# Turning q and k with 64x64 products on four quarters of the array, k loaded in whole rows, in an attention and feed-forward kernel with a re-sequenced plan

## The chip, the cores and the metric

The kernel runs on one core of a Trainium2 chip. The metric is the device time of one execution in microseconds (us). Before the change, three runs gave 1478.62, 1480.76 and 1485.36 us; the median is 1480.76 us.

## What is computed

All inputs are float32: 8 batches, 12 heads, 448 positions, 64 elements to a head. The attention's output is laid out as 3584 tokens of 768 and goes through a bilinear feed-forward layer.

```python
def rmsnorm(x, g):
    rms = np.sqrt(np.mean(x * x, axis=-1, keepdims=True) + 1e-06)
    return x / rms * g
q_n, k_n = (rmsnorm(q, g_q), rmsnorm(k, g_k))
scores = scale * np.matmul(q_n, k_n.transpose(0, 1, 3, 2))
scores = scores - np.max(scores, axis=-1, keepdims=True)
attn = np.exp(scores)
attn = attn / (np.sum(attn, axis=-1, keepdims=True) + 1e-09)
out = np.matmul(attn, v)
...
a = x @ w_a
b = x @ w_b
return (a * b @ w_out).astype(np.float32)
```

The sizes of the last part are 3584 x 768 by 768 x 1536 (twice), and 3584 x 1536 by 1536 x 768. The weights w_a, w_b and w_out arrive as 64-bit floats, two 32-bit words to a number.

## The kernel before

**Attention.** The 96 heads are handled four at a time, in 24 groups numbered p (three to a batch). Two heads lie on partitions 0 to 63 and two on 64 to 127; each head's 448 rows are spread over 64 partitions, seven rows to a partition (NT = 7). `loads` (L414) fetches q, k and v of a group through SP's queue; group 0's q and k go half by SP and half by ScalarE (L432). q and v are stored as whole rows of a head (1792 bytes to a partition and head), k with the two heads of a pair beside each other (`p j h d`), so that its pieces are 256 bytes. `normalize` (L444) squares on ScalarE (L461), sums on VectorE (L463), and takes the power -0.5 on GpSimd (L498). q is multiplied by its factors on VectorE (`apply`, L502), which writes `qn` in k's order. k's factor isn't applied to k: it is the scale of the exponential (L592).

**The turns.** The scores need q and k with the 64 elements of a head on the partitions. `transposes` (L524) does it for each group: for k, and then for q, seven TensorE transposes of 128x128 (L537), two heads at once, into a PSUM tile `pt` (tag `sc`, two buffers, shared with the scores). ScalarE copies it into `qkT` (L542 for k; L544 for q, with the gain as scale, where it also brings the two pairs of heads apart). `turn_first` (L550) is the same for group 0, with q in two parts of four and three. There, operations called `warm` (L405), whose results are not used, keep TensorE busy while it waits.

**Scores and values.** Everything else in the attention is made of 64x64 products: four of them, on the four quarters of the array, make one step of the scores (L585), of the values (L607), of the sums over the keys (L643) or of the spreading of the reciprocals (L683, with one row). ScalarE takes the exponential of each step's scores (L591, two of 128x448).

**Feed-forward.** Weights are loaded on ScalarE's queue (L358, L361), rounded to float32 by a step on ScalarE (L247) and six on VectorE (L248 to L256), combined (L371), and kept in DRAM. The products are full-array ones (128x128): L1292 and L993 for the first two pairs of batches, and L869, L993 and L1190 for the last two pairs. Up to 905 us they stand between stretches of the attention, and behind that alone.

**What sets the order.** Each step is recorded by `op` with an engine, a cost and a key, and is not emitted at once. `Plan.run` (L132) emits them all in a sequence that is written out in the file as a packed string, ORDER. The costs in the code don't reorder anything when the kernel is built. Each engine works through its own instructions in that sequence, and semaphores connect them; SP's and ScalarE's DMA issues stand in the same sequence.

Of the kernel before, what the change touches and what calls it, by code (L numbers as in the profile page):

```python
# [20 lines left out]
def _float_of(bits):  # L21
# [11 lines left out]
    "c-rkZcYIY<n%_CMzxU3q@4l8o3WOj-G&C`Qh^UMdv5!s+C>=}!34uT$BoIIZLJJCn7}DqwOo$Mqn9u^DgIFlaQp6E)+;R5jxU+xk_d>#;yECJ+"  # L33
    "&hO{W&vR}$_nfbnbG{3a0@+K%8wrF^VuJ=IScb<m4a+dy%wvFUxS6hMOl9nDb-9-X2MiXmg)VS{-v?g*>_m{=&*i%9j@dBHa^DS;;~tBfJZQj#"
    "$IfM>!$)c9Y3~6%nhK-nsJ?gu89IC@c_}A1cMjQ|Gkf|wd3l?*lWkH-O~pD=R#rTfzOlv1Dq2N15|v-G-U-XgE4Z@POG_XFTuaj-tq_*1fQ9+_"
    "`S6E-U;I`6qRN}_#*O(!71!s_hmw+&#U-mRZ@DNC@5gZN;stXR&<|k!*@A*Kr^%WMQtl$9P+nR_l+~-h-3QQZSKV&dGjI2fFX!LfSxa_6UF~*w"
    "dnddzr}i@JhV!-d&X2ai_V?dEw(V`GaY2JpRSBEq&3iV(zI|Qy!`^RpeX|?h-S~%HyT978i>&<uYCo^#*1*>C>T3E<73{3Nw0%ddbNitW8V(+O"
    "?+~0ma0(7Iz?=K_zj^pi@bck59;&N9xc95N{rf7vsINR*_t~B^?_S+=bPqI2jfXdWvh$up4Lf%pk~Zwyacb{|hWcX%kM6DCTVH=D<goA1#|?1M"
    "UEg3HI9R7`S7GnA-SEd<yLRz6zk(a^IsJU=f3@3Dv-SG+YuLZOaplUD-+y-X<~6u{`FGXU@2a)y)t9bSU#h++S6}*Axbz8kfnNOV;-?p`UB7<e"
    "n)d0HZ?9ds5>a*eTy@olUwrs+Rm~?CYR+G&Ie)&Yrs}e@>XQrA7f+l!aqc5>zWUVh_fP-%+mqF&zd3d4KTe!HcjChj&mB8<?1L}Q9y|NqvFbBN"  # L40
    "PhG2FS1+ADd8GP6qj2in`Rb3V4jp;FvGL5m{pax`jg5^LzW(}nW8=}IUsl~bdZg;`na>V39IU#2;6T+0cIh%eqkQq=p$kxd3^pGDWgi@dx)TlX"
    "?$LKQ!0wFzH@|>)ptijBSoPKF<GUI!m4C8rdrcLTLFtxrH6WH%!ztKx`t)W{HpsAXLt%AALq*|R`wLgSTV4)jg>cO>;R>v$v|wq;g{8~RE&XUU"
    "4$s080*e+ef<+4f@)y7YuwFgzD%_Y0i{TYQX4Ot+ByT1G$jyPA=`cNeS{7tawE(8TWXPOCNJd7+#0*AA`l2+FHlD!SkeUK1$(BW6G>jTeM^Yfe"
    "harKNUW6Biz>vW(gqVrg03h)>fM?;EXP<?qo$%C?5dGv60FMuXL1Z96f9Ti0A0aB~`v?IC^mz~-><zsifZpVOfSx^j_PC#Rr*I!*-R?!|T{=VO"
    "P5>R_As#HVLx&DXzCCG2NNigIF>RntYk=q|h>mmvv}y(65tN36(9jSH0YCBkhyq}{!EJ$Q0vI|)so4yYOJ>X<dATGfXU6n5a!GdK2XnGL(?Fam"
    "X47dPWWl7&Ns|QNAPuIIY176{ojPt@Ue>tDxmi;o6H+ElOvzYB^<)5HeCFiLBA7IO%$PiW^w?ZFb;-+Pri@A+nG9pe2pBzbM4mch=<uAO!?N`k"
    "U&_jQQ7;=Vq-aS)ha?RjHF)Tdmy(hOCyiV@c;tu$Y`Bp4!my;oml6lR@cavjV}3h$*vP~r-IX{vF-=eh36DK1Ii!9dKK|>+fBg*KcaSu&|A7Ae"
    "2R_noz#~#Weo)_s<N*V33>Y8^{rdG29~Gf*-$!~05A}TF{s#y3<hfqm6MFVYNa&l;=ixpHeG+;n^nM`WfnE;`?9+?u{lI<q^-#De&aMe^0>?Q;"
    "t|N$jg}cSL4q|(u*Ifeb5!+qh`EK1fp2G{>NH{`B`{08^AEBK{@DTz5d})C5AmTJo;5njkl%uUV8i?em-|ypo&r{w*If3dXZrT+0?I0Z@Qj_Oe"
    "dSn>Sg?POj2X0&kgMhX})d&PT4N~Tb-U927@bg@lmm&?YgRna2s(J@(vk1W+>I>n5@j=~gj#?N{RL4lY4Lk5Qa0ExgIqLIqG{Msy!Ml1mY7(Of"  # L50
    "zI_XPkRt^ZNOKPlgc0z$Z9u8PY9~m+Nkh{Ku+TrZB6#Bb2`6M3WfHOljD5_uPe}?%o{)^B(#FI2j8QMcSfIn{urnjz#Aq0P^wZ%-5N9Yf96oq3"
    "=``JclB4e(p!IzHiMkW}pFjHCo_e|m$j+Vc{L^jg>gwok_RwojU44dbrL|9OhblNf=*>Z!E33|Kc?&j?lLN@{P3w;g+^~M#x^0Ko^{?4d|5asO"
    "ZRMW+8`rF<Tn}%p>$i66)_!6sytSpG3@X>0DJw0lJ*kwhD?PTh^vKq-!=>eLprm+p$?D?u#c$RXuPw$y>EUux4p++hY$;n=QMq~L<~KJLZ`%08"
    "ijpUaijS{?!a}GzTv%4TW!1`}BB+PuD_8E`wQT3|wFR#gEbCpcdUXM8Syfd`DvHR;#U+cEpIVM>@#+=JUx!si4Q~|fTeWZ*T~Sbg;5!PIZKvIr"
    ")GV1_IRC9h`J0#Lzn1^nviySl`E<$RZWSw*E?=~CUg5%d2f8m<u;A5#1>KkIp^N7)nzLx(+udGyb^a?=y<XiiXYSm}O|v%6er5KoSu~;NjGno<"
    "3rpwZ&%JjRw%6w5<mBy{Icw(3nK^m$W>P%kU#Xru2WD61=HzwGnZ7P}ZP%Qs*;A*MWRq@h6ivyxcS_FW$=SI%+1bmo^E%~c@5r8i?=+a3-DS=k"
    "I$?Ily!6b8xs%fu-^|STf|fyg`n=-w%%Taa(kHF>xYNWmC`f-jef;<-shO#hCQZU8Oh`#jPtSymw2ZXmw9MptQZq8%d3nNw)CuWvX=!mVHg!KY"
    "W(?PE%%~9~M~!SZeEjhAaWE`3W!UEA)Rg4pamn~djZGdpcIcQfW5*1Q9g{VB%BWb#hKX&nvvRVs+9t(hCJy1#Vv;6}OG-^jNr@TP2BYg`h)#_h"
    "5&8588u28JY&EPEg)s6Q{N~ZHkYGxO_=6GK6ZcWC+je)wjn+0TGa(_Embj&=z%aDcyI40TU`)%V%pd|IT!BzfB#GcAfK^#IXlk1fV`)UZp@yrb"
    "X*J!NuG*R!s^cqGRXtWm6;s!(sk&d+@KcS~RozroL)W~jYPvh${zMSN>S7p%TUSjrL{<IxQq_3PquRtUm|qX*0m~C_F<aLHn&H!I&DYWG)tIH5"  # L60
    "CNnjixv>;9n69^HNZsvochs0|=~x}=%)}y5(+n+Mw{WZ>7Spin@hVCjf_OeN(1}GcW`D*|u2wAE(4%zS)bBP7Q#TEt!Q7f*-lMs(@C>L()WZzz"
    "o*+*az$rJ<k4K7bw!y;vfuR{JO|#-Pz0j~#EeOGMvy-k{;Y>AHfH4zc;*kn7r-Y)`wqbU*kd5WG!Y#ueYIwY!j?AOmx}h__7OF8%&>V57go>tQ"
    "hRJk~9*0FS^E2i}_J-C`XBNIymDxx<$jvZ~P^O~Z$VkOf*))HJjCG&S#5Jm0cAVu8_`B(*S9c>Tx7$Qx1oc6Ek+0UlVuqh--hkU1@AfiV^|*ue"
    "wtWaIa1%Xd#-TE*2hFarPG}n~ENEwB!Mq)HuWs8Gdee_{s*PgZjTS*K2aSQ+-$R0qPnOX*yq)MEUd2?Loa|6!fwhq=V#>VadQp<(q*#Sf$*J(V"
    "EU2O^icAz`S!9oBQN$z~(NuxBm`gT^gKDBF@-EsoSWl4XXc8G2sfa`&7`_lfLcj~e_Sjv*!g_QHvpa_R!R>+ecBpN)vb_;rFs)F_!c;Ilm>BIm"
    "c3WZ#Ivx@l7=B$3Pz_@bRU+-d1rC=h4kJr)nl9I9CsRTc#plx%hts2g0urW+(4&Vahy?Ip>%uEM&s)@FaF@<;4n`^E6p<IHAW-VyfC@46F$yj`"
    "KsnCj$h~s#B<2Zb8=hXAz;W?Z#&fGf-zY(dix7nHy96bahKKWfD9?L&zbDKihS-Le=gm&MS8SylJa)9c<Yy7QOA~p^(N0ht4(6n?%OT55;bfk3"
    "w&w7ZM#FL_q1aC19lXSWDo`HJb3utkEd+_D8c!)N@JbBtq!twoDmVoy#mY`uawv$%cwFFcQjnqqi4z!B9TJO?TpTZ;`jm4~Dp9_*Kt&|X^VC5V"
    "B*{@;jG|}^bTDlvI;hO?Jg4FJHR-AlD>4D$Ogybc3x%O9#)&4=d0rA-ydv;I8(t8p7{qZ>he(~R1qX5$MTye2s9gomDN!f^&rn6Gv_lDkVyN7F"
    "HqSw6d)Y-LS-};gfquX#nMz6&MVbO*3hF1jB&Q*Wf-3wLNjuvrk{}1Q6sRFnM_WmG2m=#ot4LVnC@R%ii9&_~DlAe(Xkr+RZswevgl34vH3>bg"  # L70
    "VNF6^qS{tuLH|k^xPl>g1q^U!v?x=VS48IxUUtREyu~BF7Od1%lthUZ3?!ur953@hi*hnYRlu@KB77|26r#UfBN8zfN9Yo)#-!Fk7Aj#)MII$e"
    "6p;yP#JlokmmK5b9S%twEr=5D<armteBt;A%A;4Dk|4HGsEmwMifQGNIjOaSlVy$*c_$|jj*7vGQF!=a2d9Mda%)Z!NDm^*W>=2r$d2+@RibFI"
    "t)sCKM~o88%P7JjUZkIdP;XSYKf>ej2f{+Vp1aydc)Y~+*>=FTy|&-B?GXI(#l!@Be%s@vt=z5Lcw)H&p`7KVo&?kG<{=T$w#Rgbg<H6H`YbQr"
    "t$nR+F;W+z{FY`IF*JB~gy>Y$eO`~@)~o>4Nw|g^zc(~^Y^Zjm<)K!17dNv4xMjzq^K64LCs896H6j|qeN2{|E~nS!l-v%diuRHMflw*H{3erp"
    "5^)L+4AbaVAjn~^FehjjAiP_mm_ocrjBuc#j3|oV0UoeH<Ya@xLK<8=^;4f8;|?Q`Ix%eBKsa=g1M5ryOJWQXE?CB5S<3NErEha1@bhW(J5v3_"
    "l99iv82K@ZlYemS2LW<F!WiG5r!DLBj?W+?{LcygY|!A{G}Y8^w_86YO;<A@1hbd~|FgaWge|xPP2;ARxpl!UlopWNwC~_?XS;<?TgFX)VSfu2"
    "?i|u4&a`==Nxx=nAkE*+TEO>YZ?Z<y?^ny>E$rrTvtH0b1DX+<hPP+P|8OIBJFv(Pbu#&(zW(cR^K(kizZa+6560lWi`*Q?^m{>1n`69bnKs?c"
    "&!*P=Y8t^EgXZfF3bZ9(n$iA(*^Jt}a%%_xcTk5rfWO~vqcw}xl9kQhEfk?eoZI@*zme2G#jf*{p#3Py|NCxBe(avx40dOVk-vvUeo8(5X$JcF"
    "$@WY8f7R%}m_Fnu#wS19O!_5*e`!DCG$jA`=q5iQb@BtJ$uG(GOZ(@w{|1Mt{hR"
# [68 lines left out]
def kernel(  # L148
# [126 lines left out]
    def fast_body(ld, wk, ps_s, ps_o, ps_mm, dram):  # L275
# [7 lines left out]
        STS, XS = 2, 9  # L283
        WARM, SPLIT = 4, ((0, 4), (4, NT))
# [129 lines left out]
        def loads(p, nm):  # L414
# [4 lines left out]
            def emit():  # L419
                x = ld.tile([P, NT, 2, D] if nm == "k" else [P, 2, NT * D], FP32, tag=nm, name=nm + "_sb", bufs=2 if nm == "v" else 1)  # L420
                for w in range(2):
                    pair = src[b, h0 + 2 * w:h0 + 2 * w + 2]
                    nc.sync.dma_start(x[low_high[w]], pair.rearrange("h (p j) d -> p j h d" if nm == "k" else
                                                                     "h (p j) d -> p h (j d)", j=NT))
                xs[nm, p] = x
            if p == 0 and nm != "v":
                def begin():
                    xs[nm, p] = ld.tile([P, NT, 2, D] if nm == "k" else [P, 2, NT * D], FP32, tag=nm, name=nm + "_sb", bufs=1)

                def half(w):  # L430
                    pair = src[b, h0 + 2 * w:h0 + 2 * w + 2]
                    queue[("SP", "ACT")[w]].dma_start(  # L432
                        xs[nm, p][low_high[w]], pair.rearrange("h (p j) d -> p j h d" if nm == "k" else "h (p j) d -> p h (j d)", j=NT))
                op(None, 0.0, -11, begin, [], [f"{t}/{w}" for w in range(2)], new=[t])
                for w in range(2):
                    op(("SP", "ACT")[w], 0.7, -10, lambda w=w: half(w), [], [f"{t}/{w}"], kb=350)
                return
            op("SP", 1.28 if nm != "k" else 1.4, p - (1.8 if nm == "v" else 2.0), emit, [f"firsts{PREP}"] if p >= HELD else [], [t], new=[t],
# [5 lines left out]
        def normalize(p):  # L444
# [20 lines left out]
            def front(n):  # L465
# [10 lines left out]
                def times():  # L476
                    if n == 0:
                        qns[0] = wk.tile([P, NT, 2, D], FP32, tag="qn", name="qn")
# [1092 lines left out]
```

## Time and profile before

The profiled execution took 1483.82 us, 3.1 us more than the median of the runs; its span, the time from the first to the last instruction, is 1482.0 us, so 1.8 us lie around it. Its granted TensorE clock was 0.997 of the full one.

| what | from the profile |
|---|---|
| TensorE (PE) busy | 1459.8 us, 98% of the span |
| VectorE (DVE), ScalarE (ACT), GpSimd (POOL) busy | 987.5, 437.9, 323.0 us |
| k turned: L537, 161 matmuls of 128x128 | 21.9 us, 276 ns mean of one |
| q turned: L537, 161 matmuls | 21.6 us, 274 ns |
| ACT takes k (L542) and q (L544), 23 each | 906 and 1010 ns each |
| VectorE applies q's factors (L502), 23 | 1233 ns each |
| DMA packets under 512 bytes | 62564 of 188883 |

How to read it: "busy" of a group is the time in which at least one of its instructions was running, without what overlaps an earlier one, and "mean ns" is the length of one from start to end. Matmuls overlap: one begins to stream while the one before it is still draining, so many instructions of 540 ns can fit in a time that is far shorter than their sum. PEld is the loading of weights, which has its own row. The records count a float32 product twice: the program has 672 score products, and the trace 1344 matmuls and 1344 weight loads of that line. The transposes are counted once (161 = 23 groups of 7). "Idle before" is the time an engine stood still ahead of that group, and behind the arrow stands what released it.

### The profile page before, as it was taken

The page shows a single profiled execution, that of the slowest core. Times are in us where ns is not written, and L with a number is a line of the kernel's source. Part 1 is how long each engine was busy: PE and PEld are TensorE (multiplying, and loading weights), DVE is VectorE, ACT ScalarE, POOL GpSimd, SP SyncE. Part 2 cuts the span into 40 slices and gives each one's busy share as a digit, 9 for nine tenths or more (in the row PEclk, how much of TensorE's full clock was granted, in tenths as well). Part 3 has the DMA queues.
Part 4 walks back from the last instruction along what each step waited for, and adds up shares of the span by engine and source line. Part 5 has one row for each costly group of instructions (what it writes and reads, how often), then busy time and mean ns, then how long its engine had stood idle before and what let it go on. Part 6 is the DMA issues. An engine that isn't in the chain of part 4 may idle for free.

```text
span 1482.0 us, 21059 instructions
## 1 busy us (share of the span) xinstructions
PE 1459.8 (98%) x7886; PEld 960.0 (65%) x7886; DVE 987.5 (67%) x1575; ACT 437.9 (30%) x792; POOL 323.0 (22%) x175
## 2 busy tenths in 40 slices
PE   8999999999999999999999999999999999999998
PEld 5433444555445555555544445799998899999898
DVE  5987799888766233334658765467677766776786
ACT  5878652111464000000257771011111011111100
POOL 3336541120233001101155551011120001111000
PEclk9999999999999999999999999999999999999999
DMA  9885567554443455554656544555555755555464
GB/s 226 221 235 168 123 164 210 187 186 169 159 120 89 155 170 161 178 170 149 180 156 154 128 132 149 165 170 155 161 168 180 251 172 166 159 151 158 160 197 144
DMA packets 188883, 247.99 MB, mean 167 GB/s; under 512 B 62564, under 2 KB 161380, under 8 KB 182116
## 3 DMA queue, kind: packets, MB, share of 16 engines
q1 hardware_dynamic: 159652, 192.61, 45.4%
q10 hardware_dynamic: 29120, 53.94, 10.9%
q8 instruction: 65, 1.06, 0.3%
q14 instruction: 46, 0.38, 0.1%
HBM read 188.35 MB, written 57.93 MB: 166 GB/s over the span
## 4 chain that ended last, share of the span: by engine, by line
PE 84%; DVE 2%; DMA 1%; issue 0%; ACT 0%; SPq 0%; DVEq 0%
PE pq L1292 24%; PE dg L869 17%; PE po L993 16%; PE da L869 6%; PE o L607 5%; PE sc L585 5%; PE a L1190 2%; PE g L1190 2%; PE pt L537 1%; PE b L1190 1%; PE e L1190 1%; PE d L1190 1%; PE su L643 1%; DMA ti<-kept_t 1%; DMA kept_o<-st 0%; DVE x L736 0%
## 5 line engine op out<-in xcount | busy, mean ns | idle before, releaser
L1292 PE MATMUL pq<-x,st 128*128 128x448 f32 x1008 | 384.8, 542 | 2.5 <-DVE t L1333 2.4
L1292 PEld LDWEIGHTS pq<-x,st 128*128 128x128 f32 x1008 | 190.9, 191 | 191.9 <-issue 177.2
L591 ACT ACTIVATE ET<-sc,ms 128x448 f32<-128x448 f32 x336 | 191.0, 637 | 80.3 <-PE sc L585 63.6
L498 POOL TENSOR_TENSOR ms<-ms,expo 128x14 f32<-128x14 f32 x47 | 141.0, 3003 | 117.6 <-DVE ms L496 103.6
L869 PE MATMUL dg<-dT,st 128*128 128x224 f32 x672 | 165.1, 353 | 0.0
L993 PE MATMUL po<-st,hT 128*128 128x384 f32 x492 | 164.2, 488 | 0.0
L869 PE MATMUL dg<-x,st 128*128 128x224 f32 x672 | 163.3, 353 | 0.2 <-DVE dF L916 0.2
L585 PE MATMUL sc<-qkT 64*64 64x448 f32 x1344 | 153.1, 543 | 6.4 <-ACT ET L591 3.4
L607 PE MATMUL o<-ET,v_sb 64*64 64x448 f32 x1344 | 149.3, 540 | 0.0
L897 POOL TENSOR_TENSOR hT<-dF 128x448 f32<-128x448 f32 x42 | 47.1, 1136 | 423.1 <-DVE dF L892 323.0
L993 PEld LDWEIGHTS po<-st,hT 128*128 128x128 f32 x492 | 92.6, 190 | 64.4 <-issue 4.6
L869 PEld LDWEIGHTS dg<-x,st 128*128 128x128 f32 x672 | 126.6, 190 | 2.4 <-DVE dF L916 1.2
L869 PEld LDWEIGHTS dg<-dT,st 128*128 128x128 f32 x672 | 126.6, 190 | 1.4 <-issue 0.2
L621 POOL TENSOR_TENSOR sum<-sum,ET 128x896 f32<-128x896 f32 x40 | 89.0, 2225 | 159.8 <-DVE sum L621 83.2
L869 PE MATMUL da<-x,st 128*128 128x224 f32 x504 | 118.4, 353 | 0.0
L585 PEld LDWEIGHTS sc<-qkT 64*64 64x64 f32 x1344 | 46.3, 132 | 89.8 <-issue 41.3
L607 PEld LDWEIGHTS o<-ET,v_sb 64*64 64x64 f32 x1344 | 49.8, 133 | 72.7 <-issue 64.5
L869 PEld LDWEIGHTS da<-x,st 128*128 128x128 f32 x504 | 94.5, 190 | 1.1
L892 DVE TENSOR_TENSOR dF<-dF 128x896 f32<-128x896 f32 x84 | 92.9, 1106 | 2.5
L621 DVE TENSOR_TENSOR sum<-sum,ET 128x896 f32<-128x896 f32 x60 | 65.3, 1088 | 35.5 <-POOL sum L621 29.2
L882 ACT COPY dt<-da 128x224 f32<-128x224 f32 x84 | 29.1, 346 | 197.5 <-PE da L869 87.1
L993 PE MATMUL po<-st,fin 128*128 128x384 f32 x252 | 86.7, 492 | 0.0
(151 smaller groups left out, 1663.8 us busy)
## 6 DMA issues: line engine op xcount, KB each, us to landing
st<-kept_o SPq DMA_DIRECT2D x28, 1152.0 KB
st<-kept_s SPq DMA_DIRECT2D x84, 320.0 KB
kept<-st ACTq DMA_DIRECT2D x12, 1344.0 KB
st<-kept SPq DMA_DIRECT2D x12, 1344.0 KB
st<-kept SPq DMA_DIRECT2D x84, 192.0 KB
ti<-kept_t SPq DMA_DIRECT2D x48, 288.0 KB
kept_s<-ds SPq DMA_DIRECT2D x30, 448.0 KB
v_sb<-in_v_dram SPq DMA_DIRECT2D x48, 224.0 KB
```

Of the source, the lines that this page charges most:

```text
L498: lambda: nc.gpsimd.tensor_tensor(msf(), msf(), expo[:, 0:2 * NT * (b - a)], ALU.pow), [], names)
L585: nc.tensor.matmul(t[low_high[w], e, 0:S], lhsT=qkTs[p][low_high[e], 1, j * P + w * D:j * P + (w + 1) * D], rhs=qkTs[p][low_high[e], 0, w ...
L591: nc.scalar.activation(E[:, e], scs[p, j][:, e, 0:S], AF.Exp, scale=rs[p][:, 1, 2 * j + e:2 * j + e + 1])
L607: nc.tensor.matmul(os_[p][low_high[e], w, 0:S], lhsT=xs["v", p][low_high[w], e, j * D:(j + 1) * D], rhs=ETs[p, j][low_high[w], e], start=( ...
L621: two[e].tensor_tensor(sums[p], sums[p] if j > 1 else ETs[p, 0], ETs[p, j], ALU.add)
L869: nc.tensor.matmul(to(), lhsT=W(w), rhs=t(), start=not more and k == 0, stop=k == len(terms) - 1, skip_group_check=True)
L882: nc.scalar.copy(part(0), a())
L892: take("DVE", 1.09, lambda: V.tensor_tensor(F[to], F[to], F[other], ALU.add), allF(other), allF(to), lock=True)
L897: lambda: two[e].tensor_tensor(C(i, n), F[g][:, 0:S], F[g][:, S:2 * S], ALU.mult), allF(g),
L993: nc.tensor.matmul(held["po"][:, 0:HALF], lhsT=a[0]()[:, c], rhs=sts[beta, 12 + place_of[f]][:, c], start=(c == 0), stop=(c == MH - 1))
L1190: nc.tensor.matmul(held[bank], lhsT=x()[:, c], rhs=y(c), start=(start and c == 0), stop=(stop and c == MI - 1), skip_group_check=True)
L1292: nc.tensor.matmul(banks[bank][:, 0:S], lhsT=sts[at][:, f, c * P:(c + 1) * P], rhs=quads[x][:, c], start=(start and c == 0), stop=(stop an ...
```

## The change

- The turns become products of a 64x64 block with the identity, on the four quarters: for each of the seven j, each half of the partitions w and each head h of the pair, one matmul with the block as weights and a 64x64 identity streamed (`quarter_turns`). A turn is 28 products in place of 7 transposes, 48 turns in all.
- k is loaded in whole rows, as q is. `qn`, `pt` and `qkT` are laid out by pair and head, so ScalarE's copies read two runs of 448, and the copy of q no longer reorders. Scores and the exponential's scale follow the new order of indices.
- ORDER is another string. Among other moves, ScalarE's first load of w_out's words (L358) now stands behind the two squares of q, and group 0's v (SP) behind group 1's q.
- Tiles that later reuse k's buffer get the shape of q's. The inner factors (L1118 on) keep their parts under a key of two numbers.

```diff
@@ loads: q, k and v
-                x = ld.tile([P, NT, 2, D] if nm == "k" else [P, 2, NT * D], FP32, tag=nm, name=nm + "_sb", bufs=2 if nm == "v" else 1)
+                x = ld.tile([P, 2, NT * D], FP32, tag=nm, name=nm + "_sb", bufs=2 if nm == "v" else 1)
...
-                    nc.sync.dma_start(x[low_high[w]], pair.rearrange("h (p j) d -> p j h d" if nm == "k" else
-                                                                     "h (p j) d -> p h (j d)", j=NT))
+                    nc.sync.dma_start(x[low_high[w]], pair.rearrange("h (p j) d -> p h (j d)", j=NT))
@@ apply
-                qns[p] = wk.tile([P, NT, 2, D], FP32, tag="qn", name="qn")
+                qns[p] = wk.tile([P, 2, NT, D], FP32, tag="qn", name="qn")
...
+        def quarter_turns(t, x, j0, j1):
+
+            for j in range(j0, j1):
+                for w in range(2):
+                    rows = low_high[w]
+                    for h in range(2):
+                        nc.tensor.matmul(t[low_high[h], w, (j - j0) * D:(j - j0 + 1) * D], lhsT=x[rows, h, j * D:(j + 1) * D],
+                                         rhs=ident[rows, rows], start=True, stop=True)
@@ transposes
-                    t = pts[p, n] = ps_s.tile([P, 2 * 512], FP32, tag="sc", name="pt")
-                    x = xs["k", p] if n == 1 else qns[p]
-                    for j in range(NT):
-                        nc.tensor.transpose(t[:, j * P:(j + 1) * P], x[:, j].rearrange("p h d -> p (h d)"), ident)
+                    t = pts[p, n] = ps_s.tile([P, 2, 512], FP32, tag="sc", name="pt")
+                    quarter_turns(t, xs["k", p] if n == 1 else qns[p].rearrange("p h j d -> p h (j d)"), 0, NT)
...
-                        nc.scalar.copy(qkTs[p][:, 1], pts[p, 1][:, 0:2 * S])
+                        nc.scalar.copy(qkTs[p][:, 1].rearrange("p (w t) -> p w t", w=2), pts[p, 1][:, :, 0:S])
...
-                        nc.scalar.activation(qkTs[p][:, 0].rearrange("p (w j t) -> p w j t", w=2, j=NT),
-                                             pts[p, 0][:, 0:2 * S].rearrange("p (j w t) -> p w j t", w=2, j=NT),
+                        nc.scalar.activation(qkTs[p][:, 0].rearrange("p (w t) -> p w t", w=2), pts[p, 0][:, :, 0:S],
                                              AF.Copy, scale=gain[:, 0:1])
@@ scores
-                        nc.tensor.matmul(t[low_high[w], e, 0:S], lhsT=qkTs[p][low_high[e], 1, j * P + w * D:j * P + (w + 1) * D],
+                        nc.tensor.matmul(t[low_high[w], e, 0:S], lhsT=qkTs[p][low_high[e], 1, w * S + j * D:w * S + (j + 1) * D],
                                          rhs=qkTs[p][low_high[e], 0, w * S:(w + 1) * S], start=True, stop=True)
...
-                                         scale=rs[p][:, 1, 2 * j + e:2 * j + e + 1])
+                                         scale=rs[p][:, 1, e * NT + j:e * NT + j + 1])
```

## The prediction

> **What bounds the kernel now.** I read the page's first part and its chain, then the waits of TensorE behind the head, the groups with shapes kept apart, and two stretches of the timeline.
>
> ```profile
> PE 1459.8 (98%) x7886; PEld 960.0 (65%) x7886; DVE 987.5 (67%) x1575; ACT 437.9 (30%) x792; POOL 323.0 (22%) x175
> PE 84%; DVE 2%; DMA 1%; issue 0%; ACT 0%; SPq 0%; DVEq 0%
> ```
>
> TensorE is the engine that ends the kernel. The stretch table says where: 669.99 of 670 us busy from 235 to 905, 567.35 of 568 from 905 to 1473, but 205.9 of 215.9 from 19.1 to 235. So a microsecond of TensorE's own work counts in full behind 235 us; before that VectorE (181.6) and ScalarE (154.7) are nearly as full, and it may turn into a wait.
>
> ```profile
> PE sc L585 <- ACT ET L591: 3.4, 6, 1.2
> PE pq L1292 <- DVE t L1333: 2.4, 1, 2.4
> PE sc L585 <- ACT qkT L544: 1.9, 1, 1.9
> ```
>
> These are TensorE's longest waits behind 19 us. From one matmul's start to the next, less its own streaming, I find 14.6 us lost between 19 and 235 us (1.6 of it a half clock behind the wait at 220; some hidden from the view by the draining of the matmul before), 0.2 from there to 905, and 1.0 after. More than that a new sequence can't win back there.
>
> **What a turn costs.** First the rows of the transposes, the scores, and ScalarE's and VectorE's steps beside them:
>
> ```profile
> L585 PE MATMUL sc<-qkT 64*64 64x448 f32 x1344 | 153.1, 543 | 6.4 <-ACT ET L591 3.4 <-ACT qkT L544 1.9 <-ACT qkT L542 0.6
> L502 DVE TENSOR_TENSOR qn<-q_sb,ms 128x896 f32<-128x896 f32 x23 | 28.4, 1233 | 8.7 <-POOL ms L498 8.0 <-DMA v_sb<-in_v_dram 0.7
> L544 ACT ACTIVATE qkT<-pt,gain 128x896 f32<-128x896 f32 x23 | 23.2, 1010 | 9.1 <-PE pt L537 9.0
> L537 PE MATMUL pt<-ident,k_sb 128*128 128x128 f32 x161 | 21.9, 276 | 0.0
> L542 ACT COPY qkT<-pt 128x896 f32<-128x896 f32 x23 | 20.8, 906 | 24.3 <-PE pt L537 24.0
> ```
>
> Then the timeline about 22 us and about 88 us (start, length, engine, line, count):
>
> ```profile
> 21.34 0.21 PEld L585 LDWEIGHTS sc<-qkT 64*64 64x64 f32 x8 [1.36 <-ACT ET L591]
> 22.14 0.15 PEld L643 LDWEIGHTS su<-ET,ones 64*64 64x64 f32 x4 [0.22 <-issue]
> ...
> 87.15 0.93 PE L607 MATMUL o<-ET,v_sb 64*64 64x448 f32 x8
> 88.01 0.98 PE L537 MATMUL pt<-ident,k_sb 128*128 128x128 f32 x7
> 88.83 0.93 PE L537 MATMUL pt<-ident,qn 128*128 128x128 f32 x7
> 89.69 1.74 PE L607 MATMUL o<-ET,v_sb 64*64 64x448 f32 x16
> ```
>
> Single starts in the trace give the steps: a 128x128 transpose starts 0.109 us after the one before it, so a turn streams for 7 x 0.109 = 0.764 us. Four 64x64 products of 448 columns start within 0.02 us, and the next four 0.375 us later. The last four of L607 start at 87.52 and are through at 87.90, but the turns begin at 88.01; the last transpose is through at 89.59, and L607 begins at 89.69. Going over to full-array work costs 0.11 plus 0.06 in which the first weights lie bare, and back 0.09 plus 0.05: 0.31 us for a round trip that holds turns alone. Round a full product it is 0.37, as the first 128 columns of weights take 0.10.
>
> A new turn is 28 products of 64x64 with 64 columns: seven times four quarters. How many passes is one? The scores' 672 products have 1344 records, `warm`'s 36 of 128x128 have 72, the transposes one each: an ordinary float32 product passes twice, a transpose once. [...] if one were enough, the turn would be half. With two there are 14 steps of four quarters. A step's streaming is 64/448 of 0.3733 plus the 0.0022 that each length shows on top: 0.0555 us. The turn is 14 x 0.0555 = 0.78 us, against 0.764. The quarters win four and lose it again: half the columns, twice the passes. One pass would make it 0.39.
>
> Are the weight loads hidden at so short a step? [...] the eight loads at 21.34 span 0.06 more than four do at 22.14, so a load holds its quarter for 0.055, a step is 0.11, a turn 1.55. In the trace each quarter's next load starts 2 ns behind the start of the matmul in it, same row group, and the steps stay at 0.375[...]. I take the row: 0.78. The ends are 0.39 and 1.55. Feeding is no limit that the row shows: 32 records went to the queue in 0.13 us between two semaphore waits at 464.7, 4 ns each, and a turn's 112 records in 0.78 us are 7 ns each.
>
> **The change, part by part.**
>
> - *Turns, 46 behind the head*: 46 x (0.78 - 0.764) = +0.7 us, of which 0.4 (24 turns, groups 12 to 23) lie where TensorE is full.
> - *Going between modes*: in the built programs' order the transposes stood beside feed-forward products or alone in 9 stretches of their own. Behind the head there were 44 full-array stretches and now there are 42, as the new sequence splits the products into more. Up to the long stretch at 200 us 18 become 12; behind it 26 become 30. The second half costs 4 x 0.37 = +1.5; the first saves 6 x 0.35 = -2.1, where waits may take it up.
> - *ScalarE's copy of q*: from 1010 toward the 906 of k's copy, 23 x 0.1 = 2.4 us off an engine that isn't last. *`apply`*: it writes whole runs now, between 1233 (no change) and 1088 (a plain add of 896, L621): 0 to 3.3 us off VectorE; I take half, 0.07 each. Behind 235 us TensorE covers both: 0. Before it these two engines end TensorE's waits, and 11 of each are 1.1 + 0.8 = 1.9 us less: -1.9 (0 if the waits come from elsewhere).
> - *k in whole rows*: 24 x 1792 pieces of 256 bytes become 6144 of 1792. Behind the head k's landing holds ScalarE's squares for 11.7 us in all and TensorE never: 0.
> - *Shapes, keys, index of scales*: the same instructions: 0.
> - *The head.* Here k's landing ends a wait of TensorE:
>
> ```profile
> 2.27 0.63 ACTq L358 DMA_DIRECT2D hraw<-in_moe_w_out_dram  x1
> 5.63 1.04 ACT L473 ACTIVATE sq<-q_sb 128x512 f32<-128x512 f32 x2 [1.94 <-DMA q_sb<-in_q_dram]
> 10.78 0.95 ACT L461 ACTIVATE sq<-k_sb 128x896 f32<-128x896 f32 x1 [4.11 <-DMA k_sb<-in_k_dram]
> 12.99 1.18 DVE L479 TENSOR_TENSOR qn<-q_sb,ms 128x512 f32<-128x512 f32 x2
> 19.02 1.74 PE L585 MATMUL sc<-qkT 64*64 64x448 f32 x16
> 20.13 2.90 ACT L591 ACTIVATE ET<-sc,ms 128x448 f32<-128x448 f32 x5 [0.69 <-PE sc L585]
> ```
>
> q's SP half lands at 5.40, k's at 10.55: from 6.5 on, w_out's packets of 6144 bytes run and k's pieces of 256 fall from 200 to 20 in half a microsecond. With those words behind the squares of q (ScalarE's end at 6.67), and with 128 rows in place of 896 pieces, k should land near 6.8 (q's half took 0.9 us of packets and 0.9 to land). Then: k's squares wait for VectorE's second sum of q (7.64) and end at 8.65; the sum of k ends at 9.75; q's factors apply from 10.0 in place of 12.99. GpSimd's power for k runs from 10.3 to 13.3 (was 16.1). TensorE's `warm` after k's turn ends by 9.5, the q turns and their `warm` take the same 3.6 us as from 15.43 to 19.02, so the scores start near 14.6. The words now land later: issued at 6.7 and 7.7, 0.79 MB each at about 0.27 MB a us behind 2 us of start, at about 14.4. The step L247, which stands ahead of the first exponential on ScalarE, runs to 16.1, and the exponentials start there in place of 20.13: -4.0 us. Past what else was it moved? Group 0's v is now issued behind q of group 1, which waits for `apply` (11.2): by about 20.5 it has landed, and L607 needs it near 21. k of group 1 follows on SP and lands near 23, with its turn due at 22.6, since it stands earlier now; behind that turn wait the values and scores. I take -4.0 + 0.5 = -3.5, between 0 (all of it lost to those landings) and -4.4.
> - *The rest of the new sequence*: most steps move by one or two places. It can save 8 of the 14.6 us (VectorE's and ScalarE's share stays) or cost 6. The wait at 220.16 keeps the same producers in the same order on VectorE, so I take nothing here, and count the -2.1 above as half taken up: -1.0.
>
> Sum: +0.7 + 1.5 - 1.0 - 1.9 - 3.5 + 0 = -4.2. Against the profiled execution 1483.8 - 4.2 = 1479.6; the median of the runs lies 3.1 lower: 1476.5, said as 1476.
>
> **The rivals.** A measurement here can tell about 0.5% (7.4 us: below 1473.4, above 1488.2).
>
> - *Turns as costed, head won* (0.5): 1468 to 1484, by the waits.
> - *One pass or some faster form* (0.18): the turn is 0.39 to 0.45, 46 x 0.35 = 16 us less, 12 if a part before 235 us becomes waiting: 1459 to 1465. For it speaks that the streamed operand is an identity, as with transposes; against it `warm`, an identity too, which passes twice.
> - *Slower: loads lie bare on a quarter* (0.18). [...] 46 x 0.77 = 35 us, 1511; half bare, 1494. It decides from a step of 0.063 us on (46 x 14 x 0.0067 = 4.3 us, the whole gain), and is slower by over 0.5% from 0.074. Against it stand the steps at 448 and 128 columns; for it, that no row has a step of 64 columns.
> - *The new order waits more* (0.14): group 1's late v and k stall the start, VectorE holds TensorE as at 220: nothing won, 1481 to 1489.
>
> Faster by over 0.5%: 0.18 + 0.22 of the first case = 0.40. Slower: 0.17 of the third + 0.03 of the fourth = 0.20. Between: 0.40. For 8 in 10 the range leaves out the far end of the third case: 1459 to 1491; the likeliest case alone is 1468 to 1484.
>
> **What would show it.** Two records for each product of a turn (2576 for the 46); four quarters within 0.03 us, 0.055 us from step to step, 0.78 a turn. The first exponential near 16, k's squares near 7.7, no half clock about 10 us. ScalarE's q copy near 906. 42 full-array stretches behind the head and still no wait between 235 and 905. I am wrong if a step is 0.03 or 0.07 and more, or if the waits before 235 us change by over 8 us.

## The result

After the change 20 runs have a median of 1478.03 us (1476.97 to 1481.48); before it, 20 runs beside them on the same chip 1483.16 us. The ratio is 0.9968, 95% interval 0.9961 to 0.9975: some 5 us, 0.3%. A second set of 21 runs later gave 0.9977 (0.9968 to 0.9985). The forecast was 1476.

The profiled execution took 1479.91 us (span 1478.1), 1.9 us over the median. First, from the profile after, the page's busy line, and the shares in the chain of work that ended last, followed back from the end:

```profile
PE 1461.7 (99%) x10238; PEld 967.3 (65%) x10238; DVE 986.4 (67%) x1575; ACT 437.6 (30%) x792; POOL 328.9 (22%) x175
PE 94%; DVE 2%; DMA 1%; ACT 1%; issue 1%; POOL 1%; SPq 0%; ACTq 0%; POOLq 0%; DVEq 0%
```

TensorE is busy for 1.9 us more, in a span 3.9 us shorter: the kernel got faster by waiting less, not by doing less. The groups (line, engine, operation, tiles, shapes, count | busy us, mean ns | idle before):

```profile
L500 DVE TENSOR_TENSOR qn<-q_sb,ms 128x896 f32<-128x896 f32 x23 | 26.9, 1169 | 3.4 <-POOL ms L496 3.2
L528 PE MATMUL pt<-ident,qn 64*64 64x64 f32 x1344 | 25.3, 220 | 2.5 <-ACT rec L662 1.1 <-DVE qn L500 0.8 <-issue 0.6
L528 PE MATMUL pt<-ident,k_sb 64*64 64x64 f32 x1344 | 25.0, 219 | 0.0
L549 ACT ACTIVATE qkT<-pt,gain 128x896 f32<-128x896 f32 x23 | 23.2, 1008 | 35.3 <-PE pt L528 35.2
L547 ACT COPY qkT<-pt 128x896 f32<-128x896 f32 x23 | 20.8, 906 | 11.0 <-PE pt L528 10.8
```

48 turns of 28 products have 2 x 1344 records: each product passes twice. ScalarE's copy of q takes as long as before (1010), k's too; `apply` fell from 1233 to 1169. In the trace of single starts, a step of four quarters follows the one before it by 0.0583 us (starts at 23.362, 23.421, 23.479, 23.537), so a turn streams for 14 x 0.0583 = 0.817 us.

The head, in the timeline after:

```profile
5.44 0.36 ACTq L359 DMA_DIRECT2D hraw<-in_moe_w_out_dram  x1
7.43 0.95 ACT L459 ACTIVATE sq<-k_sb 128x896 f32<-128x896 f32 x1 [1.00 <-DVE ms L483]
7.44 1.04 PE L528 MATMUL pt<-ident,k_sb 64*64 64x64 f32 x56
14.91 1.73 PE L587 MATMUL sc<-qkT 64*64 64x448 f32 x16
16.02 2.90 ACT L593 ACTIVATE ET<-sc,ms 128x448 f32<-128x448 f32 x5 [0.87 <-PE sc L587]
```

k's squares no longer wait for k, and scores and exponentials start 4.11 us earlier than before. TensorE's longest waits from 19 to 235 us are now:

```profile
PE sc L587 <- ACT ET L593: 2.6, 3, 1.7
PE pt L528 <- ACT rec L662: 1.1, 1, 1.1
```

The wait for L1333 at 220 us and the half clock behind it are gone.

Where the time went is best read as a lead: how much earlier the same piece of work starts than before. In the two profiles it is 4.1 us at the first score, 8.5 where the feed-forward products of the second pair have begun (222 us in after), 6.0 where the last stage begins (947), and 4.4 at the last product. Before's profile is one execution, of 1483.82 us; a lead says what happened in an execution, the ratio what the kernel gains.

### The profile page after: what moved, and what is told of

Read it like the earlier page. It is cut to its first block, busy times and chain, and to the rows that moved or that the text cites. A ratio compares the mean times of both kernels' runs of the same rounds, so it can differ in the third digit from the quotient of the medians.

```text
span 1478.1 us, 25741 instructions
## 1 busy us (share of the span) xinstructions
PE 1461.7 (99%) x10238; PEld 967.3 (65%) x10238; DVE 986.4 (67%) x1575; ACT 437.6 (30%) x792; POOL 328.9 (22%) x175
## 4 chain that ended last, share of the span: by engine, by line
PE 94%; DVE 2%; DMA 1%; ACT 1%; issue 1%; POOL 1%; SPq 0%; ACTq 0%; POOLq 0%; DVEq 0%
PE pq L1294 24%; PE dg L871 17%; PE po L995 17%; PE o L609 8%; PE sc L587 8%; PE da L871 6%; PE pt L528 3%; PE a L1192 2%; PE g L1192 2%; PE su L645 2%; PE e L1192 1%; PE b L1192 1%; PE d L1192 1%; PE warm L409 1%; ACT ET L593 1%
## 5 line engine op out<-in xcount | busy, mean ns | idle before, releaser
L623 DVE TENSOR_TENSOR sum<-sum,ET 128x896 f32<-128x896 f32 x60 | 65.0, 1084 | 37.3 <-POOL sum L623 20.6
```

The lines of the kernel that those rows point to most:

```text
L623: two[e].tensor_tensor(sums[p], sums[p] if j > 1 else ETs[p, 0], ETs[p, j], ALU.add)
```

## The experiments

Theory 1: the head and fewer waits up to 235 us make the gain; turns on quarters cost more than the transposes did, and some is given back later. Theory 2: the turns win by themselves. Theory 3: the new sequence wins by itself.

The table comes from the traces. "Own work" is the time from the first score product's start to the last product's start, less what single starts came late by over 0.16 us ("waits"). The three kernels with before's products in before's order (e4, e9, e10) differ from before by +0.5 to +1.3 there, so it is known to about 1 us.

| kernel | ratio to before (95%) | first exp | own work | waits to 125 / 235 / 905 / end | full-array stretches |
|---|---|---|---|---|---|
| before | 1 | 20.1 | 0 | 7.2 / 7.4 / 0.2 / 1.0 | 44 |
| after | 0.9968 (0.9961-0.9975) | 16.0 | +3.0 | 5.5 / 4.3 / 0.7 / 2.0 | 42 |
| e1 new code, old sequence | 1.0025 (1.0015-1.0034) | 17.8 | +3.0 | 7.6 / 7.5 / 0.4 / 0.7 | 43 |
| e2 old code, new sequence | 0.9985 (0.9977-0.9993) | 15.8 | +6.1 | 4.5 / 3.8 / 0.7 / 2.0 | 64 |
| e3 words first again | 0.9988 (0.9976-1.0000) | 19.9 | +2.9 | 4.5 / 3.8 / 0.7 / 2.2 | 42 |
| e4 old, words late | 0.9984 (0.9975-0.9993) | 15.9 | +0.5 | 10.4 / 7.3 / 0.2 / 0.3 | 44 |
| e5 turns twice | 1.0324 (1.0300-1.0348) | 18.1 | +43.3 | 3.1 / 6.5 / 7.0 / 4.8 | 42 |
| e6 last stage in old sequence | 0.9967 (0.9954-0.9980) | 16.0 | +2.8 | 3.4 / 4.4 / 0.7 / 0.3 | 42 |
| e7 old sequence from 222 us | 0.9971 (0.9961-0.9981) | 16.0 | +3.4 | 4.2 / 4.3 / 0.9 / 0.3 | 43 |
| e8 mixed | 0.9957 (0.9942-0.9973) | 15.7 | +0.5 | 3.4 / 4.3 / 1.2 / 0.5 | 38 |
| e9 old, x ahead | 0.9988 (0.9980-0.9997) | 21.1 | +0.8 | 4.0 / 4.0 / 0.6 / 0.5 | 44 |
| e10 old, three moves | 0.9972 (0.9962-0.9981) | 16.1 | +1.3 | 5.5 / 3.8 / 0.6 / 0.3 | 44 |
| e11 mixed again | 0.9961 (0.9947-0.9974) | 15.4 | +1.2 | 4.5 / 4.4 / 1.2 / 0.7 | 38 |
| e12 after again | 0.9977 (0.9968-0.9985) | 16.5 | +3.0 | 3.5 / 4.3 / 0.7 / 2.0 | 42 |

Line numbers of a changed kernel can differ by a few from those of the listing.

### Code and sequence apart (e1, e2)

e1 is the changed file with before's ORDER; e2 is before's file with after's ORDER (and the two-number key of the inner factors, which that sequence needs).

> The changed code (quarter turns, k in whole rows, apply in whole runs) emitted in the sequence of before; w_out's first words stand ahead of the squares of q again. Theory 1 (the gain is made by the head and by fewer waits up to 235 us; the turns themselves lose): 46 turns cost 46 x 0.053 = +2.4 us, 43 full-array stretches in place of 44 give -0.3, apply -0.5, and the head wins only what whole rows win against the words' packets, about -2: -0.4 us against before, that is 1482 to 1484. Theory 2 (turns on quarters win by themselves, as they need no change of mode): -4 us or more, 1479 or less. Theory 3 (the new sequence alone makes the gain): +2 us, 1485.

Measured: 1485.62 us, 3.4 more than before (1482.22). The head won 2.3 us, and own work took back 3.0: 2.4 of it are 46 turns x 0.053. In the profile the last product comes 1.1 us later than in before's; that execution of before took 1.6 us more than the median here, so the two figures lie closer than they look. Theory 1 had said 1482 to 1484, so it was too low, and 1485 is the figure of theory 3. The new code alone is slower; theory 2 falls.

> The code of before (transposes of the full array, k in pieces of 256 bytes) emitted in the sequence of after. Theory 1: the sequence takes turns out of the full-array stretches, which only quarter turns make cheap; with transposes there are 63 such stretches behind the head in place of 44: 19 x 0.31 = +5.9 us, against -4 for fewer waits and -3 for the words sent later: about -1 us, 1480 to 1485. Theory 3 (the sequence alone makes the gain): -5 us, 1478. Theory 2 (the sequence is good for quarter turns alone, and wins nothing in the head): +3 to +6 us, 1486 to 1489.

Measured: 1480.41 us, -1.8. Waits fell as in after, but the sequence breaks the transposes out into 64 full-array stretches: 6.1 us of own work for 20 more, 0.30 each. That is what quarter turns are good for: not a cheaper turn, but a turn that can stand anywhere among 64x64 products. Neither half makes the gain: theory 3 had said -5 us, and the sequence alone gets 1.8 of the 3.2 to 5.1 us that the whole change won in its two sets of runs.

### The head (e3, e4)

e3 moves one instruction of after back; e4 moves the same one in before:

```diff
@@ sequence of after, ScalarE (e3)
+hraw (w_out's first words)
 squares of q, parts 0 and 1
-hraw (w_out's first words)
@@ sequence of before, ScalarE (e4)
-hraw (w_out's first words)
 squares of q, parts 0 and 1
+hraw (w_out's first words)
```

> The kernel after, with ScalarE's first load of w_out's words put back ahead of the squares of q. Theory 1 (both the words and the pieces held k): k in whole rows gets a larger share beside the words than the pieces did, lands about 8.5 us in place of 6.8, and the first exponential comes at 17.5 to 18.5: +2 us on after, 1480. Rival (the words alone held k): first exponential at 20, +4 us, 1482. Rival (the pieces alone did): 16.0, 1478.

Measured: 1481.50 us, first exponential at 19.88; the kernel is within 0.7 us of before (1482.22), so most of the gain hangs on the head. k in whole rows landed at 9.73, and its turn starts 1.1 us earlier than before (10.81) but 2.3 us later than in after (7.44). The scores start 3.9 us later than in after; the other 1.6 us is TensorE's clock. First k's turn in e1 and in e3, which have the same head, then the table by stretches of e3 (window, length, busy PE, PEld, DVE, ACT, POOL, granted clock, DMA share, GB/s):

```profile
9.23 1.04 PE L526 MATMUL pt<-ident,k_sb 64*64 64x64 f32 x56 [1.83 <-DMA k_sb<-in_k_dram]
9.73 1.53 PE L526 MATMUL pt<-ident,k_sb 64*64 64x64 f32 x56 [2.02 <-DMA k_sb<-in_k_dram]
```

```profile
10.00:12.50 2.50, 2.50 (x61) 2.38 (x51) 1.69 (x3) 0.74 (x1) 0.35 (x1) 0.52 0.61 182
12.50:15.00 2.50, 2.50 (x42) 2.36 (x45) 0.68 (x2) 0.33 (x2) 2.50 (x1) 0.80 1.02 415
```

TensorE had idled for 2.0 us before k's turn, and then ran at half clock for some 3.4 us. In e1 k landed at 9.23, the idle time was 1.8 us, and the granted clock stayed at 1.00: from k's turn to the first score e1 takes 7.5 us, as after does, and e3 9.0. Half a microsecond of landing decided 2 us of start.

> The kernel before, with only ScalarE's first load of w_out's words moved behind the two squares of q; k stays in pieces of 256 bytes. Theory 1: the pieces ran at 200 packets in half a microsecond until the words came, so k lands near 7.5 and the first exponential comes near 16.8: -3.3 us on before, 1480. Rival (the pieces alone are slow): 19.5 to 20, -0.5 us, 1482.5. If the start's gain is lost to later waits of VectorE and ScalarE anyway: the first exponential is early and the end within 1 us of before.

Measured: 1480.19 us, 2.0 under before, first exponential at 15.90. In pieces k lands at 8.18 (expected 7.5), and that is early enough: moving the words makes the head by itself, and whole rows add nothing once the words are late (in the profiles with single turns 15.8 to 16.1 with pieces, 15.4 to 16.5 with rows). With the words first, rows did help: by 2.3 us at the first exponential in e1's profile, by 0.3 in e3's. But e4's lead of 4.2 us is down to 0.5 at 125 us (that execution took 1482.59, 2.4 us over the median, so the runs kept more of it). In e4's timeline, and then in before's:

```profile
89.87 0.95 ACT L459 ACTIVATE sq<-q_sb 128x896 f32<-128x896 f32 x1 [2.45 <-DMA q_sb<-in_q_dram]
90.73 0.99 ACT L542 ACTIVATE qkT<-pt,gain 128x896 f32<-128x896 f32 x1
91.77 0.61 PE L583 MATMUL sc<-qkT 64*64 64x448 f32 x4 [2.11 <-ACT qkT L542]
```

```profile
92.22 0.95 ACT L461 ACTIVATE sq<-q_sb 128x896 f32<-128x896 f32 x1 [2.28 <-DMA q_sb<-in_q_dram]
94.12 0.98 PE L585 MATMUL sc<-qkT 64*64 64x448 f32 x8 [1.95 <-ACT qkT L544]
```

ScalarE stands at the squares of group 5's q, which has not landed. Behind them waits the copy of group 4's turned q, long ready, and for that the scores wait. Before has the same wait and keeps its clock; in e4 it is 0.16 us longer, 6.8 us of half clock follow, and by 102 us 2.0 us of lead are gone. The first 1.7 had gone by 66 us, in part through new waits for q's factors (1.3 us at 29 us) and for v's landing (0.6 at 59).

### What the new sequence removes (e9, e10)

In before, about 219 us, VectorE and GpSimd do this:

```profile
218.17 1.08 DVE L621 TENSOR_TENSOR sum<-ET 128x896 f32<-128x896 f32 x1
219.17 3.04 DVE L736 TENSOR_TENSOR x<-x,rec 128x448 f32<-128x448 f32 x2
219.34 2.39 POOL L621 TENSOR_TENSOR sum<-sum,ET 128x896 f32<-128x896 f32 x1 [8.78 <-DVE sum L621]
222.80 3.79 PE L1292 MATMUL pq<-x,st 128*128 128x448 f32 x5 [2.37 <-DVE t L1333]
```

One of the two L736 takes 0.62 us, the other, begun beside GpSimd's add, 2.51. Of 36 such steps four take 2.5 us in before, and one in after; each of these began while GpSimd's add was running. The rest take 0.61 to 0.64. The add began 0.37 us ahead of the step and ends at 221.73, and the step 0.5 us later; a step of q's factors that began 0.2 us ahead of such an add (150.77) took 1084 ns, as one alone does. Not every step inside an add is held: one of L736 on `inv` in place of `rec`, begun 0.3 us behind an add's start (120.39), took 0.615. That the add holds the step is read from these times; by what means is not shown. L1333 stands behind the step on VectorE, and TensorE waits for L1333. e9 moves the two steps ahead of the add:

```diff
@@ sequence of before, VectorE (e9, e10)
+x<-x,rec (two)
 sum<-ET
-x<-x,rec (two)
@@ sequence of before, ScalarE (e10; also the move of e4)
-squares of q, group 5
 copy of q, group 4
+squares of q, group 5
```

> The kernel before, with one move in its sequence: the two steps of VectorE that scale a batch's attention (L736, x<-x,rec) near 219 us stand ahead of VectorE's add of two exponentials (L621), and no longer behind it, where the second of them runs beside GpSimd's add for 2.5 us in place of 0.62. Theory 1 (VectorE is held by GpSimd's add, and TensorE then waits 2.4 us for L1333 and falls to half its clock for some 3 us): the wait at 220 shrinks to under 0.8 us and the half clock goes, -3 to -4 us from 235 us to the end, 1479. Rival (TensorE's products or the order of VectorE's own steps set that wait): the wait stays over 2 us and the end is within 0.5 us of before.

e9's timeline:

```profile
216.62 1.16 DVE L734 TENSOR_TENSOR x<-x,rec 128x448 f32<-128x448 f32 x2
217.69 1.08 DVE L619 TENSOR_TENSOR sum<-ET 128x896 f32<-128x896 f32 x1
219.36 4.78 PE L1290 MATMUL pq<-x,st 128*128 128x448 f32 x12 [0.52 <-DVE t L1331]
```

By single starts the wait of 2.5 (2.37 in the view) is 0.7 (0.52), the half clock is gone, and over this place the lead grows by 2.8 us. Across the runs e9 is 1.8 us faster than before (1481.20 to 1483.04), half of what was expected. Why the runs show less than the place itself is not shown; the waits ahead of it vary from execution to execution (e9's profile starts its scores 1.0 us later than before and leads by 1.6 at 125 us, with nothing changed up to there). In after, too, the two steps stand ahead of the add: they run from 212.32, the add from 215.53.

> The kernel before, old code throughout (transposes of the full array, k in pieces of 256 bytes), with three moves in its sequence: w_out's first words behind the squares of q; the two scaling steps near 219 us ahead of VectorE's add; and on ScalarE the squares of group 5's q (they wait for its landing at 92 us, and the take of group 4's q waits behind them) behind that take. Theory 1 (the gain lies in a few places of the sequence and needs no quarter turns): -4.2 us at the first exponential, about -3 still at 125 us, -6 to -7 from 235 us to the end, 1475 to 1477. Rival (the lead is used up by ScalarE and VectorE wherever it is let through, so that only the place at 220 us pays): -3 to -4 us at the end, 1479.

Measured: 1479.02 us, ratio 0.9972: three moves in before's sequence, with none of the new code, give about what the whole change gives. In its profile the lead is 4.7 us at 125 and 8.3 at 222; that execution took 1475.69, the shortest of its 16 (up to 1482.17), so the median shows half of it. That median, 4.0 us under before, is the rival's figure, and no more than e4's 2.0 and e9's 1.8 together: that the third move adds something, as theory 1 had it, shows in the profile alone. There, q's squares behind the copy:

```profile
87.54 1.01 ACT L542 ACTIVATE qkT<-pt,gain 128x896 f32<-128x896 f32 x1
88.84 0.95 ACT L459 ACTIVATE sq<-q_sb 128x896 f32<-128x896 f32 x1 [0.28 <-DMA q_sb<-in_q_dram]
```

### The price of a turn, and what is given back (e5 to e8)

e5 loops twice over j in `quarter_turns`. e6, e7 and e8 follow after's sequence to a point and then emit what is left in before's order: from the last stage on (e6), or from 222 us on (e7, e8). e8 also turns groups 12 to 23 by transposes, with k in pieces.

```diff
@@ e5
-            for j in range(j0, j1):
+            for j in [*range(j0, j1)] * 2:
@@ e8, for p >= 12
+                        for j in range(NT):
+                            nc.tensor.transpose(t[:, j * P:(j + 1) * P], x[:, j].rearrange("p h d -> p (h d)"), ident)
```

> The kernel after, with each turn's 28 products issued twice into the same tile (the second time writes the same values). Theory 1 (a turn's own time lies on TensorE's path): 48 x 0.817 = 39.2 us more TensorE work. Behind 235 us it counts in full: 24 x 0.817 = 19.6 us; up to there part may go into the 9 us of waits that are left, so 10 to 18 us. The whole: +30 to +38 us on after, 1508 to 1516. Rival (turns on quarters run beside other quarters' work, so that a turn costs less than its own steps): under +20 us, 1498 or less.

Measured: 1529.92 us, 51.9 more than after's 1478.03 on another chip. Own work grew by 40.3 us (46 x 0.817 = 37.6; the other 2.7 are not accounted for), so a turn lies on TensorE's path in full and hides nothing; the rival falls. My own figure was low as well: waits did not take part of it up, they grew by 8.7. More than that are stops inside or behind a doubled turn, eleven of up to 2.6 us and 10.4 us together, that the waits view puts down to "issue", no other engine; in after there is one of 0.6 us. One of them, and the row of the page for the DMA queue named "instruction" in after and in e5 (packets, MB, share):

```profile
840.41 1.55 PE L528 MATMUL pt<-ident,qn 64*64 64x64 f32 x89 [1.40 <-issue]
```

```profile
q8 instruction: 83, 1.36, 0.4%
q8 instruction: 104, 1.70, 0.5%
```

The 21 packets more, of 16384 bytes each, are 64 bytes for each of the 5376 instructions that e5 has more, so I take them to carry the program itself. In all ten stops of over 0.15 us TensorE goes on 1.3 to 1.6 us after the end of such a packet, and so it does in after; less than 3% of e5's time lies so far behind one. So these stops look like waits for the program, which such short products may use up faster than it comes; no run was made to test that.

> The kernel after up to its last step of attention, and from there all operations that are left in the sequence of before. Theory 1 (the new sequence waits more in the last stage): the lead over before stays at the -6.0 us that it has when that stage starts, in place of -4.4 at its end: -1.5 us on after, 1476.5. Rival (these waits come with the lead itself, as VectorE's or DMA's work of that stage is then late by comparison): no change from after, 1478.

> The kernel after up to 222 us, and from there all operations that are left in the sequence of before; all turns on quarters. Theory 1: the -8.5 us of that place are kept but for 24 turns x 0.053 = 1.3 us and 5 full-array stretches more than before has there, at 0.25 each: -6 us against before, 1477. Rival (the lead at 222 us is work put off, which is to be done later): -4 us or less, 1479.

> As the kernel that follows before's sequence from 222 us on, but with transposes of the full array and k in pieces of 256 bytes for groups 12 to 23; groups 0 to 11 turn on quarters with k in whole rows. Theory 1: turns and changes of mode behind 222 us are those of before, and so are the waits: all of the -8.5 us is kept, 1474 to 1475 against 1482.5 before. Rival (the lead at 222 us is work put off): -4 us or less, 1479. If quarter turns were cheaper than transposes, this kernel would be slower than its twin with quarters throughout.

Measured: 1476.84, 1478.16 and 1474.87 us (before: 1481.79). TensorE's waits behind 905 us in after, and then in e6:

```profile
PE dg L871 <- DVE dF L918: 0.6, 1, 0.6
PE dg L871 <- DVE dt L911: 0.5, 1, 0.5
```

```profile
PE dg L869 <- DVE dF L916: 0.2, 1, 0.2
```

In all four profiles with the new sequence in the last stage and single turns (after, e2, e3, e12) the lead shrinks by 1.5 to 1.9 us there; in e6, e7, e8 and e11 it grows by 0.2 to 0.5. So the last stage's waits belong to the sequence, not to the lead. By its total time e6 can't be told from after. e8 is where its theory 1 had it, and its rival (work put off) falls; e7, 3.6 us under before, is at its rival's figure by the runs, and 5.6 under by the two profiles. From 222 us to the end e7 loses 3.2 us of its lead, e8 0.6 and the second run of e8's kernel (e11, below) 1.4, though all follow one sequence: transposes where before had them are worth 1.8 to 2.6 us over quarters there by the profiles, and 3.3 by the medians (24 x 0.053 = 1.3, and 5 fewer full-array stretches at 0.30 are 1.5).

> The mixed kernel once more (after's sequence and quarter turns to 222 us, before's sequence with transposes from there), beside the kernel after on the same chip, to tell it from that one: its six runs so far leave the intervals overlapping. Theory 1: 3 to 4 us under after, 1474 to 1475.5. Rival (the low time came from few runs): within 1.5 us of after, 1476.5 to 1478.

> The kernel after, unchanged, beside the mixed kernel. All theories: 1477 to 1479, with its profile showing whether the wait of 1.9 us at 68 us is there in each execution; if it comes and goes with the landing of a transfer, the time up to 125 us differs by up to 2 us from the first profile.

Measured: 1475.97 and 1478.81 us on one chip. The mixed kernel is some 3 us faster than after and 6 than before; eight of its nine runs (1475.04 to 1476.90) lie under all but two of after's 21. And after's second profile lacks the wait at 68 us. Here are the squares of q, on ScalarE, in the first and in the second:

```profile
68.53 0.95 ACT L459 ACTIVATE sq<-q_sb 128x896 f32<-128x896 f32 x1 [2.20 <-DMA q_sb<-in_q_dram]
66.36 0.95 ACT L459 ACTIVATE sq<-q_sb 128x896 f32<-128x896 f32 x1
```

A place like e4's is thus still in the new sequence, and costs 0 or 2 us by how the transfers fall.

## Why the prediction came out as it did

The total was right to 2 us, and the change to 1: -4.2 was forecast, from a median of three runs of before (1480.76), and -5.1 measured beside 20 runs (1483.16). The head carried most of it, as said: e3, which lacks it, is 0.7 us faster than before. But several terms were not what they measured.

- *Turns*: +0.7 was forecast, +2.4 measured. Two passes, quarters together (within 0.02 us) and hidden loads held: each quarter's next load starts 2 ns behind its matmul's start. The size was off: a step is 0.0583, not the 0.0555 scaled down from 448 columns, and 14 x 46 steps make 1.8 us of that. The slower rival would have begun at 0.063. The prediction's 0.11, an estimate of 0.055 for the load plus 0.055 for the streaming should the two not overlap, isn't seen: the next load of the same quarter overlaps the running product.
- *Modes*: 42 stretches came as counted, and 0.31 for a round trip is confirmed by e2's 0.30. Behind 235 us the lead falls by 4.1: 1.5 are waits, 1.3 the 24 turns, and the 1.3 left fits the +1.5 for four more stretches. Up to there own work grew by 0.4, with 1.2 of turns in it, so the six fewer stretches gave about 0.8, where 1.0 was counted.
- *ScalarE's copy of q toward 906*: wrong. It stayed at 1008 with the two runs. e2, in the old layout, also has 1008: the reordering had never cost anything. What is left to set it apart from k's copy (906) is its form, an activation with a scale in place of a plain copy; no run tests that.
- *`apply`, half of 145 ns for whole runs*: the number came out (-64) and its cause is wrong. With whole runs in the old sequence (e1) the mean is 1232; with the old layout in the new sequence (e2) 1170. One that runs alone takes 1088 in before and 1083 in after; each mean holds two of 1.9 to 3.0 us, which began beside GpSimd's work. So -1.9 for "waits of ScalarE and VectorE" was the wrong mechanism.
- *The wait at 220*: "keeps the same producers in the same order on VectorE, so I take nothing" was the step that failed most. The producers were the same; their neighbour on GpSimd wasn't (e9). Fewer waits up to 235 us gave 4.8 us in after's first profile and 6.8 in its second, where 1.9 had been counted.
- *Head*: -4.1 against -4.0. The words' place made it by itself (e4), as the 200-to-20 fall of the packets had let expect; the rows, to which the prediction gave a part, added nothing to that. The 0.5 for late landings wasn't needed at 21 us. It came at 68 us in one profile, at another group's q.
- *The last stage*: 0 was taken, +1.0 of waits came.
- *Feeding*, taken as no limit: one stop of 0.6 us at 135 us, of the kind seen in e5.

So the sum of -4.2 stood partly by luck, because errors met: TensorE's own work was costed at +1.2 (0.7 + 1.5 - 1.0) and is +3.0, and the waits behind 235 us grew by 1.5; against both stood 3 to 5 us of waits more than counted that went away, those at the step held beside GpSimd's add (2.51 us) among them. From the profile after: -4.1 (head) + 3.0 (own work) - 4.8 + 1.5 (waits) = -4.4, which is the lead at the last product.

## What to carry to other kernels

Before crediting a change of layout or shape with a shorter mean, split the group's instructions by what runs beside them: a mean of 1233 was 1088 alone plus two of 2.5 and 3.0 us that began during GpSimd's adds, and moving a neighbour was the whole effect. A lead won at the start can be lost where an engine's sequence has a step that waits for a transfer ahead of one that is ready: in e4's profile ScalarE stood 2.45 us at such a step, in e10's, with the two turned round, 0.28. Look for such pairs first: e10's three moves of single steps, one of them of this kind, were worth about as much here as the rewrite. A turn by full-array transposes beside full-array work is the cheaper one (0.764 us against 0.817); the quarter form pays where it saves a change of mode (0.30 us a stretch in e2).

## What was not expected of the hardware

- TensorE fell to half clock for about 3.4 us after 2.0 us of idling (e3) and kept full clock after 1.8 (e1). In the 14 profiles, behind the start and ahead of the last product, it idled eight times for 2.02 us or more (to 4.23), and 3.4 or 6.8 us of half clock followed each time; no idle time of up to 1.95 us was followed by one.
- A float32 turn of 28 quarter products (0.817 us) costs slightly more than 7 full transposes (0.764): the quarters' gain of four is spent on half the columns and twice the passes.
- VectorE writes 64-element runs (128x896) as fast as whole ones: 1088 ns (before) and 1083 (after) for one alone.
- In doubled turns, 224 records in a row, TensorE stops for up to 2.6 us, and goes on 1.3 to 1.6 us after the end of a packet of the queue named "instruction" (e5).
